# Zero-adding fillers on TensorE: 128 columns in a softmax bank instead of 256 in a free one, six softmax banks from the first unit, and another order

## The chip, the cores and the metric

The kernel runs on one core of one Trainium2 chip. The metric is the device time of one execution in microseconds (us), smaller being better. TensorE (PE in the profile) multiplies, VectorE (DVE) and ScalarE (ACT) do the element-wise work, GpSimd (POOL) builds masks, SyncE (SP) issues the DMAs. PSUM, where TensorE writes, has eight banks of 512 fp32 columns.

## The reference

Three layers on 4 batches of 576 tokens, 8 heads of 64:

```
scores = q k^T / 8, masked: heads 0-3 to the last 32 positions, heads 4-7 to every 32nd position
x  = softmax(scores) v                       (2304 x 512)
x  = mish(x w_in) w_out                      (512 -> 2048 -> 512)
out = max(x w1, x w2, x w3) w_out2           (512 -> 768 -> 512)
```

q and k come scaled up by 8, and the weights come in 64-bit words that the kernel turns into fp32 itself.

## The kernel before

Attention is cut into 48 units, 12 for each batch: a unit is three or four blocks of one pair of heads. Each unit has one PSUM bank for its whole life. It goes: mask by a matmul (`mask_mm`, L476, in the first two batches), scores (L485, 64x64 tiles of the array), row maximum on VectorE (L506), exponentials on ScalarE (L518), division on VectorE (L531), transposes on TensorE (L542), copies out of the bank (L554: for the strided heads one on ScalarE and one on VectorE, from different partitions of one bank into different columns of the same tile), the product with v (L563), and the split of the result into a high and a low part of x (L581 ScalarE, L585 VectorE). For the first batch, q and k are transposed on TensorE (L409, 96 columns each) and copied out (L422 ScalarE, L424 VectorE); later batches use VectorE (L382).

The first layer (L608, `h_mm`) starts on a block of tokens as soon as its x is there, so its matmuls lie between those of the attention units. Every product runs in three passes of high and low parts. x w_out follows (`x2_mm`, L641), then a Strassen scheme for the wide layers (L826) and the last product (L943).

The order on every engine is written out by a planner at build time. `Plan.add` notes each step with a cost, its reads and its writes; `Plan.run` simulates the engines with these costs and takes, whenever an engine is free, the ready step of the best rank. Twenty seeds shake the ranks one after the other. `START` says when each engine begins in the plan's time (ns).

**Fillers.** Where the plan's TensorE would stand idle, `Plan.run` (L196 to L203) puts in matmuls of zeros. It counts one as FILL columns at 2.4 or 1.2 GHz, as its own model of the clock says for that moment (`HAM`, `HAM_COLS`), and puts in as many as end `FILL_GAP` ns ahead of the next step. Fillers are no steps of the plan: they have neither reads nor writes there. In the built program the semaphores come from the tiles that the instructions touch.

**Banks.** `ATT_BANKS` are five banks that the units take in turn. The bank acc0 is the fillers' at first, and from unit 12 (`SIXTH`) on it is the sixth bank of the units, so that unit 17 is the first to use it. From the first step of such a unit that the plan takes, no more fillers are put in (`plan.unfilled`; `fill` in L198 stays false once it is false). At the start VectorE sets the zeros that the fillers read (L1268) and clears the five banks in the order a0, a1, a2, acc1, acc2 (L1270).

Of the kernel before, what the change touches and what calls it, by code (L numbers as in the profile page):

```python
# [21 lines left out]
P = 128  # L22
# [18 lines left out]
LQ = 64  # L41
LK = LQ + STRIDE
RES = 3
ATT_BANKS = ("a0", "a1", "a2", "acc1", "acc2")
RAW_BANKS = ("h0", "acc3")
RING = dict(h=3, g=5, ev=4, wt=4, hq=10, land=6, s=6, st=8, pt=3, raw=2, qT=2, v=2)
CFG = dict(lead_conv=2.43, att_rate=1.0, att_lead=0.53, start_conv=4.96, start_step=1.17, start_unit=1.19, x2=0.0)
PASSES = ((0, 0), (0, 1), (1, 0))

START = dict(pe=1460, act=1900, dve=4360, pool=5630, sp=1000, qa=1000)  # L50
WAIT = dict(
    pe=dict(pe=0, act=200, dve=210, pool=200, sp=200), act=dict(pe=260, act=140, dve=150, pool=200, sp=150),
    dve=dict(pe=230, act=140, dve=130, pool=160, sp=150), pool=dict(pe=260, act=200, dve=200, pool=130, sp=200),
    sp=dict(pe=200, act=160, dve=160, pool=160, sp=100),
)
for waits in WAIT.values():
# [4 lines left out]
ISSUE = dict(v_load=470, tr_ld=575)  # L61
QUEUE = 200
PIECES = dict(qk_load=36, tr_ld=36, w_first=32, w_load=32)
SIXTH = 12
HAM, HAM_COLS = 10240 / 3, 3060
SMALL_MM = ("scores", "tp", "av", "qkt")
MODE = dict(scores="64x64", tpq="64x64", avs="64x64", av="128x64")
SWITCH_IN, SWITCH_OUT, SWITCH_TILED = 140, 200, 145
STAY = 2000
TABLE = dict(exps="exp", mish="mish", mish1="mish")  # L70
TABLE_LOAD, TABLE_STAY = 1400, 4000
FILL, FILL_GAP = 256, 100
ROUNDS = 5
MOVED, JITTER = (0.01, 0.03, 0.1, 0.2), (1000, 2000, 4000)
SEEDS = (2000001, 2000002, 2000007, 2000010, 2000013, 2000055, 2000060, 2000065, 2000101, 2000130, 2000162, 2000272, 2000304, 2000349, 2000351, 2000592, 2001064, 2001088, 2001199, 2001207)
COST = dict(
    act=lambda n, psum=False, ptr=False: (51 if psum else 93) + n / 1.2 + (93 if ptr else 0),
    dve=lambda n, fast=False: 69 + n / (1.92 if fast else 0.96),
# [4 lines left out]
def switch(was, mode):  # L83
    if was == mode:
        return 0
    return SWITCH_IN if was is None else SWITCH_OUT if mode is None else SWITCH_TILED


def pieces(name, cost):
    return cost / 20 if name == "v_load" else PIECES.get(name, 16)  # L90


class Queued:

    def __init__(self):
        self.held, self.sum = deque(), 0
# [13 lines left out]
class Plan:  # L110
# [6 lines left out]
    def __init__(self, filler):  # L117
        self.filler = filler
        self.name, self.eng, self.cost, self.cols, self.rank, self.emit = [], [], [], [], [], []
        self.pred, self.succ = [], []  # L120
        self.writer, self.readers = {}, {}
        self.unfilled = set()

    def add(self, name, eng, cost, emit, reads=(), writes=(), rank=0.0, cols=0):
        i = len(self.name)
# [16 lines left out]
    def run(self, rank, backward):  # L142
        succ, pred = (self.pred, self.succ) if backward else (self.succ, self.pred)
        n = len(self.name)
        left = [len(p) for p in pred]
        ready, done = [0.0] * n, [0.0] * n
        free = dict.fromkeys(self.ENGINES, 0.0) if backward else dict(START)
        later = {e: [] for e in self.ENGINES}
        now_ready = {e: [] for e in self.ENGINES}
        for i in range(n):  # L150
            if not left[i]:
                heappush(later[self.eng[i]], (0.0, i))
        order, wire, busy, last, mode, fill, count = [], 0.0, {}, None, None, True, 0
        queued = {e: Queued() for e in self.ENGINES}
        table = "mish" if backward else "exp"
        while count < n:
            now, e = min(
                (free[e] if now_ready[e] else max(free[e], later[e][0][0]), j)
                for j, e in enumerate(self.ENGINES) if now_ready[e] or later[e]
            )  # L160
            e = self.ENGINES[e]
            while later[e] and later[e][0][0] <= now:
                i = heappop(later[e])[1]
                heappush(now_ready[e], (rank[i], i))
            if e == "pe" and last is not None:
                def worth(entry):
                    name = self.name[entry[1]]
                    same = MODE.get(name) == mode
                    return entry[0] - STAY * same, entry[1]

                r, i = min(now_ready[e], key=worth)
                now_ready[e].remove((r, i))
                heapify(now_ready[e])
            elif e == "act":
                def late(entry):
                    t = TABLE.get(self.name[entry[1]], table)
                    return entry[0] + TABLE_STAY * (t != table), entry[1]

                r, i = min(now_ready[e], key=late)
                now_ready[e].remove((r, i))  # L180
                heapify(now_ready[e])
            else:
                i = heappop(now_ready[e])[1]
            cost = self.cost[i]
            if e == "act":
                t = TABLE.get(self.name[i], table)
                cost += TABLE_LOAD * (t != table)
                table = t
            if e in ("sp", "qa"):
                now = max(now, queued[e].room(pieces(self.name[i], cost)))  # L190
                free[e] = now + ISSUE.get(self.name[i], DMA_ISSUE)
                wire = max(wire, now + (0 if backward else DMA_START)) + cost
                queued[e].put(wire, pieces(self.name[i], cost))
                done[i] = wire + (DMA_START if backward else 0) + DMA_END + LATE.get(self.name[i], 0)
            else:
                if e == "pe":  # L196
                    t, w = free[e], int(free[e] // HAM)
                    fill = fill and not backward and self.name[i] != "x2_mm" and i not in self.unfilled  # L198
                    while fill and t + (c := FILL / (2.4 if busy.get(w - 1, 0) >= HAM_COLS else 1.2)) + FILL_GAP <= now:
                        busy[w] = busy.get(w, 0) + FILL  # L200
                        order.append(-1)
                        t += c
                        w = int(t // HAM)  # L203
                    last, was, mode = self.name[i], mode, MODE.get(self.name[i])
                    cost += switch(was, mode)
                    if not backward:
                        w = int(now // HAM)
                        busy[w] = busy.get(w, 0) + self.cols[i]
                        cost *= 1 if busy.get(w - 1, 0) >= HAM_COLS else 2
                done[i] = free[e] = now + cost  # L210
            order.append(i)
            count += 1
            for j in succ[i]:
                wait = WAIT[self.eng[j]][e] if backward else WAIT[e][self.eng[j]]
                ready[j] = max(ready[j], done[i] + wait)
                left[j] -= 1
                if not left[j]:
                    heappush(later[self.eng[j]], (ready[j], j))
        return order, done, max(done)
# [10 lines left out]
    def order(self):  # L230
# [3 lines left out]
        rank = self.rank  # L234
        for seed in (*SEEDS, None):
            end, order, done = self.settle(rank, ROUNDS)
# [12 lines left out]
def build_plan(k, B, H, S, D, DM, FF, FF2, wide):  # L249

    plan = Plan(lambda: k.fill())
    add = plan.add
    nc = k.nc
# [10 lines left out]
    act, dve, mm = COST["act"], COST["dve"], COST["mm"]  # L264
# [166 lines left out]
    def unit(n, i, u, tiles, b, hp, local, r, rv):  # L431
        rk = unit_rank(n)
        nt = len(tiles)
# [1 line left out]
        C = LK if local else LQ  # L435
        M = LQ if local else RK
        rows = P if local else LQ + RK
        tag = ATT_BANKS[n % len(ATT_BANKS)] if n < SIXTH else (*ATT_BANKS, "acc0")[n % 6]
        bk = ("bank", tag)
        sb = ("s", ring("s"))  # L440
        pb = ("pt", ring("pt"))
# [20 lines left out]
                return a[:, st:st + LK]  # L462
            return a[:, NJ * RES * tl:NJ * RES * tl + width(tl)]

        if tag == "acc0":
            plan.unfilled.update(range(len(plan.name), len(plan.name) + nt + 1))
        on_pe = b < PE_MASK
        if on_pe:
            def mask_mm():
# [592 lines left out]
def sparse_attention_moe_kernel(  # L1062
# [13 lines left out]
    nc = tc.nc  # L1076
# [30 lines left out]
    for i in range(RING["g"]):  # L1107
# [14 lines left out]
    banks = {tag: psum.tile([P, 512], F32, name=f"bank_{tag}")  # L1122
             for tag in ("a0", "a1", "a2", "h0", "acc0", "acc1", "acc2", "acc3")}
# [125 lines left out]
    zero = x[:, 0, KC - 1, NT - FILL:]  # L1249

    def fill():
        nc.tensor.matmul(banks["acc0"][:, :FILL], lhsT=zero[:, :P], rhs=zero, start=True, stop=True)

    bufs = dict(work, s=s_t, pt=pt_t)
    env = SimpleNamespace(
        nc=nc, fill=fill, x=x, x2p=x2p, out=out, ident=ident, m_first=m_first, m_res=m_res, m_first_r=m_first_r, m_res_r=m_res_r, ident_r=ident_r,
        bank=lambda tag: banks[tag], wt=lambda r: wt[r][:], words=split_words,
        stage=lambda s: slot_tile(s, [P, 1024], U32), open_slot=lambda s: slot_tile(s, [P, 2, 512], F32R),
# [5 lines left out]
    plan = build_plan(env, B, H, S, D, DM, w_in.shape[1], w1.shape[1], wide)  # L1264
    order, _ = plan.order()
    with tc.manual_schedule():
        nc.scalar.preload_act_table_set("exp_and_others")
        nc.vector.memset(zero.bitcast(F32), 0.0)  # L1268
        for tag in ATT_BANKS:
            nc.vector.memset(banks[tag][:], 0.0)  # L1270
# [33 lines left out]
```

## Time and profile before

| | |
|---|---|
| median of 3 runs | 749.46 us (748.99 to 749.92) |
| the profiled execution | 747.73 us, its span 745.7 us |
| TensorE busy | 736.7 us (99%), 5192 matmuls |
| VectorE, ScalarE busy | 519.8 us (70%), 400.0 us (54%) |
| granted TensorE clock over the span | 0.994 |

All times inside the trace count from the start of the span. A matmul is busy from its issue until its last result is written, so consecutive matmuls overlap and a short stop of the array does not show as idle time. The granted clock is 1.00 at 2.4 GHz and 0.50 at 1.2 GHz.

### The profile page before, as it was taken

How to read it: one execution, taken by the hardware profiler on the slowest of the kernel's cores; microseconds unless marked ns; L12 is line 12 of the kernel's file. 1: busy time of each engine (PE TensorE's matmuls, PEld its weight loads, DVE VectorE, ACT ScalarE, POOL GpSimd, SP SyncE). 2: the span in 40 equal slices, each digit the busy share in tenths (PEclk: the TensorE clock that was granted, in tenths of full speed). 3: DMA queues.
4: the chain of work that ended last, by engine and by line, in shares of the span. 5: the costliest groups of instructions: out<-in, count | busy, mean ns of one | idle time of the engine just before them, and what ended most of it. 6: DMA issues, size and time to landing. Idle time of an engine off the chain costs nothing.

```text
span 745.7 us, 14087 instructions
## 1 busy us (share of the span) xinstructions
PE 736.7 (99%) x5192; PEld 707.3 (95%) x5192; DVE 519.8 (70%) x1174; ACT 400.0 (54%) x1082; POOL 6.0 (1%) x28
## 2 busy tenths in 40 slices
PE   8999999999999999999999999999999999999998
PEld 7799987999999999999999999999999999998886
DVE  5999997893798488333886769966656854694321
ACT  5868888695656266252663747543244343353331
POOL 3000000000000000000000000000000000000000
PEclk9999999999999999999999999999999999999999
DMA  9897783443555657345681326212520441365542
GB/s 192 167 159 134 136 165 102 167 156 115 178 155 185 196 190 251 99 126 169 211 270 44 127 74 211 85 58 68 167 68 28 131 131 57 116 203 169 177 130 85
DMA packets 152212, 105.39 MB, mean 141 GB/s; under 512 B 95312, under 2 KB 145488, under 8 KB 152144
## 3 DMA queue, kind: packets, MB, share of 16 engines
q1 hardware_dynamic: 150960, 104.20, 48.8%
q8 instruction: 41, 0.67, 0.4%
q10 hardware_dynamic: 1184, 0.30, 0.2%
q14 instruction: 27, 0.22, 0.1%
HBM read 74.58 MB, written 29.88 MB: 140 GB/s over the span
## 4 chain that ended last, share of the span: by engine, by line
PE 93%; DVE 3%; ACT 2%; DMA 1%; POOL 0%; issue 0%; SPq 0%; POOLq 0%; DVEq 0%; ACTq 0%
PE bank_acc L641 27%; PE bank_a L826 21%; PE bank_acc L826 11%; PE bank_h L826 11%; PE bank_acc L943 5%; PE bank_a L943 3%; PE bank_h L608 3%; PE bank_acc L608 3%; PE bank_acc L485 1%; PE bank_h L943 1%; PE bank_a L563 1%; PE bank_a L485 1%; ACT s L518 1%; PE bank_acc L563 1%; PE bank_a L542 1%; DMA rawk<-in_k_dram 1%
## 5 line engine op out<-in xcount | busy, mean ns | idle before, releaser
L641 PE MATMUL bank_acc<-g,wslot 128*128 128x384 f32 x1152 | 210.6, 334 | 0.0
L641 PEld LDWEIGHTS bank_acc<-g,wslot 128*128 128x128 f32 x1152 | 200.5, 188 | 0.1
L826 PE MATMUL bank_a<-x,wslot 128*128 128x384 f32 x732 | 143.3, 334 | 0.0
L826 PEld LDWEIGHTS bank_a<-x,wslot 128*128 128x128 f32 x732 | 128.4, 188 | 0.0
L333 ACT CAST wslot<-wt 128x512 fp32r<-128x512 f32 (+1 forms) x86 | 50.1, 584 | 31.6 <-DVE wt L319 21.7
L674 DVE SCALAR_TENSOR_TENSOR ev<-bank_acc,ev 128x384 f32<-128x384 f32 x72 | 39.0, 552 | 37.4 <-PE bank_acc L641 35.3
L826 PE MATMUL bank_acc<-ty,wslot 128*128 128x384 f32 x324 | 64.4, 334 | 0.0
L337 DVE TENSOR_TENSOR wslot<-wt,wslot 128x512 fp32r<-128x512 f32 (+1 forms) x86 | 53.8, 637 | 6.1 <-ACT wslot L333 5.9
L826 PEld LDWEIGHTS bank_acc<-ty,wslot 128*128 128x128 f32 x324 | 56.9, 188 | 0.1
L826 PE MATMUL bank_h<-ty,wslot 128*128 128x384 f32 x240 | 48.0, 334 | 0.0
L943 PE MATMUL bank_acc<-wslot,g 128*128 128x512 f32 x180 | 44.9, 389 | 0.0
L636 DVE TENSOR_TENSOR g<-h,g 128x384 fp32r<-128x384 f32 x45 | 24.7, 554 | 25.8 <-ACT g L635 25.5
L826 PEld LDWEIGHTS bank_h<-ty,wslot 128*128 128x128 f32 x240 | 42.2, 188 | 0.0
L309 DVE TENSOR_SCALAR wt<-wt 128x512 uint32<-128x512 uint32 x56 | 23.4, 421 | 24.8 <-ACT wt L305 24.7
L943 PEld LDWEIGHTS bank_acc<-wslot,g 128*128 128x128 f32 x180 | 33.8, 188 | 6.9
L313 DVE SCALAR_TENSOR_TENSOR wt<-wslot,wt 128x512 uint32<-128x512 uint32 x56 | 38.4, 686 | 0.7
L305 ACT ACTIVATE wt<-wslot 128x512 f32<-128x512 f32 x56 | 37.5, 676 | 2.1 <-DMA wslot<-in_moe_w_dram 1.8
L319 DVE SCALAR_TENSOR_TENSOR wt<-wslot,wt 128x512 uint32<-128x512 uint32 x56 | 38.0, 683 | 0.3
L826 PE MATMUL bank_h<-x,wslot 128*128 128x384 f32 x186 | 37.2, 334 | 0.0
L608 PE MATMUL bank_h<-x,wslot 128*128 128x288 f32 (+2 forms) x168 | 35.0, 334 | 0.0
L608 PE MATMUL bank_acc<-x,wslot 128*128 128x288 f32 (+2 forms) x168 | 34.0, 334 | 0.0
L842 ACT COPY bank_acc<-bank_a 128x384 f32<-128x384 f32 x27 | 12.6, 465 | 38.6 <-PE bank_a L826 38.3
(174 smaller groups left out, 1222.0 us busy)
## 6 DMA issues: line engine op xcount, KB each, us to landing
x2p<-ev SPq DMA_DIRECT2D x72, 192.0 KB
ev<-x2p SPq DMA_DIRECT2D x72, 192.0 KB
wslot<-in_moe_w_out_dram SPq DMA_DIRECT2D x22, 512.0 KB
wslot<-in_moe_w_dram SPq DMA_DIRECT2D x18, 512.0 KB
wslot<-in_moe_w_in_dram SPq DMA_DIRECT2D x16, 512.0 KB
ty<-t SPq DMA_DIRECT2D x20, 384.0 KB
h<-g SPq DMA_DIRECT2D x24, 192.0 KB
hy<-h SPq DMA_DIRECT2D x24, 192.0 KB
```

Of the source, the lines that this page charges most:

```text
L305: nc.scalar.mul(k.wt(r2).bitcast(F32), k.words(slot)[1].bitcast(F32), 2.0 ** -111)
L309: nc.vector.tensor_scalar(out=t, in0=t, scalar1=3, scalar2=None, op0=ALU.logical_shift_left)
L313: nc.vector.scalar_tensor_tensor(out=t, in0=k.words(slot)[1], scalar=0x80000000, in1=t, op0=ALU.bitwise_and, op1=ALU.bitwise_or)
L319: nc.vector.scalar_tensor_tensor(out=t, in0=k.words(slot)[0], scalar=29, in1=t, op0=ALU.logical_shift_right, op1=ALU.bitwise_or)
L333: nc.scalar.copy(out=k.open_slot(slot)[:, 0, :n], in_=k.wt(r2)[:, c0:].bitcast(F32))
L337: nc.vector.tensor_tensor(out=s[:, 1, :n], in0=k.wt(r2)[:, c0:].bitcast(F32), in1=s[:, 0, :n], op=ALU.subtract)
L608: nc.tensor.matmul(k.bank(hb)[:, :n], lhsT=wap(("in", f), a, c), rhs=k.x[:, q, c, t0:t0 + n], start=(c == 0 and m == 0), stop=(c == KC - 1 ...
L636: add("gl", "dve", dve(n), lambda: nc.vector.tensor_tensor(out=g()[:, 1, :n], in0=Hh(), in1=g()[:, 0, :n], op=ALU.subtract), reads=[h, G0] ...
L641: nc.tensor.matmul(k.bank(f"acc{c}")[:, :n], lhsT=wap(("out", f), a, c), rhs=g()[:, q, :n], start=(first and m == 0), stop=(last and m == 2),)
L674: add("x2_add", "dve", dve(n), (lambda c=c, e=e, ab=ab: nc.vector.scalar_tensor_tensor(out=k.work("ev", e)[:, :n], in0=k.bank(ab)[:, :n], ...
L826: nc.tensor.matmul(k.bank(bank)[:, :SP], lhsT=left(i, a, pa, j), rhs=operand(p, b, pb, j, x2), start=start and n == 0, stop=n == 5, skip_g ...
L943: nc.tensor.matmul(k.bank(ab)[:], lhsT=k.g(rg)[:, a, c * P:(c + 1) * P], rhs=t[:, q, :], start=(f == 0 and m == 0), stop=(f == F2C - 1 and ...
```

## The change

- A filler has 128 columns instead of 256 (`FILL`), and may end 60 ns instead of 100 ns ahead of the next step (`FILL_GAP`). It goes into columns 384 to 511 of the bank a2, with `start=False`, so that it adds zeros there. The units use at most the first 384 columns of a bank.
- acc0 is one of six `ATT_BANKS` from unit 0 on. `SIXTH` and `plan.unfilled` go, so fillers may be put in until the first `x2_mm`. Six banks are cleared at the start: a0, a1, a2, acc1, acc2, acc0.
- The zeros are set over 128 columns of x instead of 256.
- The plan begins TensorE at 1200 ns instead of 1460, and its model of the clock has another mark (`HAM_COLS`).
- Other seeds: the order of all steps is new.

```diff
-ATT_BANKS = ("a0", "a1", "a2", "acc1", "acc2")
+ATT_BANKS = ("a0", "a1", "a2", "acc1", "acc2", "acc0")
-START = dict(pe=1460, act=1900, dve=4360, pool=5630, sp=1000, qa=1000)
+START = dict(pe=1200, act=1900, dve=4360, pool=5630, sp=1000, qa=1000)
-SIXTH = 12
-HAM, HAM_COLS = 10240 / 3, 3060
+HAM, HAM_COLS = 10240 / 3, 3700
-FILL, FILL_GAP = 256, 100
+FILL, FILL_AT, FILL_GAP = 128, 384, 60
-SEEDS = (2000001, ...)
+SEEDS = (1000001, ...)
...
-                    fill = fill and not backward and self.name[i] != "x2_mm" and i not in self.unfilled
+                    fill = fill and not backward and self.name[i] != "x2_mm"
...
-        tag = ATT_BANKS[n % len(ATT_BANKS)] if n < SIXTH else (*ATT_BANKS, "acc0")[n % 6]
+        tag = ATT_BANKS[n % len(ATT_BANKS)]
...
-        if tag == "acc0":
-            plan.unfilled.update(range(len(plan.name), len(plan.name) + nt + 1))
...
     def fill():
-        nc.tensor.matmul(banks["acc0"][:, :FILL], lhsT=zero[:, :P], rhs=zero, start=True, stop=True)
+        nc.tensor.matmul(
+            banks["a2"][:, FILL_AT:FILL_AT + FILL], lhsT=zero, rhs=zero, start=False, stop=True, skip_group_check=True
+        )
```

## Rows read from the trace of the kernel before

**Rows 1.** Stretches: length, busy us of PE, PEld, DVE, ACT, POOL, clock, DMA, GB/s

```profile
14.00:34.00 20.00, 17.95 (x301) 14.35 (x300) 18.47 (x61) 18.22 (x91) 0.00 (x0) 1.00 0.98 179
34.00:42.00 8.00, 8.00 (x87) 7.22 (x88) 5.88 (x21) 3.63 (x15) 0.00 (x0) 0.57 1.09 204
42.00:140.00 98.00, 96.94 (x1342) 86.21 (x1341) 89.74 (x279) 81.85 (x355) 0.00 (x0) 1.00 0.67 135
140.00:700.00 560.00, 560.00 (x3197) 554.48 (x3197) 387.20 (x779) 277.41 (x577) 0.00 (x0) 1.00 0.43 140
```

**Rows 2.** Waits of TensorE, 10 to 41 us: us in total, times, longest

```profile
PE bank_a L542 <- ACT s L518: 0.7, 1, 0.7
...
PEld bank_a L476 <- DVE x L585: 0.4, 1, 0.4
...
PE bank_acc L485 <- ACT qTq L422: 0.2, 1, 0.2
```

**Rows 3.** Waits of TensorE, 41 to 140 us

```profile
PE bank_acc L485 <- DVE x L585: 0.4, 1, 0.4
...
PE bank_acc L485 <- DVE qTk L382: 0.2, 1, 0.2
```

**Rows 4.** Timeline of TensorE, 0 to 20 us: start, us, instruction, [idle before]

```profile
1.18 4.00 PE L1252 MATMUL bank_acc<-x 128*128 128x256 f32 x17 [1.18 <-DVE x L1268]
5.47 0.71 PE L409 MATMUL bank_h<-ident,earlyq 96*128 96x96 f32 x3 [0.29 <-POOL s L1151]
...
9.33 0.59 PE L476 MATMUL bank_acc<-m_first_r,ident_r 128*128 128x288 f32 x1
9.85 1.83 PE L485 MATMUL bank_a<-qTk,qTq 64*64 64x96 f32 x36
...
15.77 0.41 PE L409 MATMUL bank_h<-ident,earlyq 96*128 96x96 f32 x3
...
19.46 0.40 PE L476 MATMUL bank_a<-m_first_r,ident_r 128*128 128x288 f32 x1
```

**Rows 5.** Groups of TensorE, 0 to 10 us: xcount | busy us, mean ns

```profile
L476 PE MATMUL bank_a<-m_first_r,ident_r 128*128 128x288 f32 x3 | 1.4, 539 | 0.0
L476 PE MATMUL bank_acc<-m_first_r,ident_r 128*128 128x288 f32 x3 | 1.4, 539 | 0.0
```

**Rows 6.** Timeline of VectorE, the start

```profile
0.86 0.27 DVE L1268 MEMSET x<- 128x256 f32 x1 [0.86 <-PEq L1289]
1.23 1.56 DVE L1270 MEMSET bank_a<- 128x512 f32 x3
...
6.86 0.46 DVE L424 COPY qTk<-bank_acc 128x288 f32<-128x288 f32 x1 [2.98 <-PE bank_acc L409]
```

**Rows 7.** Groups of TensorE, 40 to 140 us

```profile
L608 PE MATMUL bank_acc<-x,wslot 128*128 128x128 f32 x12 | 1.5, 275 | 0.0
L608 PE MATMUL bank_h<-x,wslot 128*128 128x128 f32 x12 | 1.5, 270 | 0.0
```

**Rows 8.** Weight loads, 40 to 140 us and then 0 to 10 us

```profile
L608 PEld LDWEIGHTS bank_acc<-x,wslot 128*128 128x128 f32 x150 | 22.9, 189 | 1.7
...
L1252 PEld LDWEIGHTS bank_acc<-x 128*128 128x128 f32 x17 | 3.7, 328 | 1.2 <-DVE x L1268 1.2
```

**Rows 9.** Timeline of TensorE, around 62 us

```profile
61.06 0.60 PE L608 MATMUL bank_h<-x,wslot 128*128 128x288 f32 x3
61.59 0.61 PE L485 MATMUL bank_acc<-qTk,qTq 64*54 64x54 f32 x16
...
63.20 0.67 PE L608 MATMUL bank_h<-x,wslot 128*128 128x288 f32 x3
63.71 0.56 PE L608 MATMUL bank_acc<-x,wslot 128*128 128x288 f32 x3
```

**Rows 10.** Waits of VectorE and of ScalarE, 10 to 140 us

```profile
DVE pt L554 <- ACT pt L554: 1.8, 5, 0.5
...
ACT pt L554 <- DVE pt L554: 1.7, 5, 0.5
```

More of the change, by code (lines that the diff above doesn't have):

```diff
@@ L63 @@
 PIECES = dict(qk_load=36, tr_ld=36, w_first=32, w_load=32)
-SIXTH = 12
-HAM, HAM_COLS = 10240 / 3, 3060
-SMALL_MM = ("scores", "tp", "av", "qkt")
+HAM, HAM_COLS = 10240 / 3, 3700
 MODE = dict(scores="64x64", tpq="64x64", avs="64x64", av="128x64")
@@ L71 @@
 TABLE_LOAD, TABLE_STAY = 1400, 4000
-FILL, FILL_GAP = 256, 100
+FILL, FILL_AT, FILL_GAP = 128, 384, 60
 ROUNDS = 5
 MOVED, JITTER = (0.01, 0.03, 0.1, 0.2), (1000, 2000, 4000)
-SEEDS = (2000001, 2000002, 2000007, 2000010, 2000013, 2000055, 2000060, 2000065, 2000101, 2000130, 2000162, 2000272, 2000304, 2000349, 2000351, 2000592, 2001064, 2001088, 2001199, 2001207)
+SEEDS = (1000001, 1000002, 1000003, 1000004, 1000009, 1000077, 1000082, 1000087, 1000142, 1000168, 1000181, 1000185, 1000187, 1000190, 1000273, 1000333, 1000373, 1000500, 1000562, 1000593)
 COST = dict(
@@ L121, in __init__ @@
         self.writer, self.readers = {}, {}
-        self.unfilled = set()
     def add(self, name, eng, cost, emit, reads=(), writes=(), rank=0.0, cols=0):
```

## The prediction

> **What bounds the kernel now.** I read the table of stretches first [rows 1]. From 140 to 700 us TensorE has no idle time and the clock is full, and the change touches no step there; between 42 and 140 it is 99% busy. So the end comes when TensorE has done its list of work: whatever it loses or gains before 42 us is lost or gained at the end, as long as VectorE, 92% busy from 42 to 140 (89.74 of 98), can follow. Before 42 us there are two losses. From 14 to 34 us ScalarE and VectorE are the tight ones (18.22 and 18.47 of 20), and TensorE waits for them, six times by name between 10 and 41 us, 2.6 us in all [rows 2]. From 34 to 42 us TensorE is busy all the time, but at a mean clock of 0.57: (1 - 0.57) x 8 / 0.5 = 6.9 us at the lower of its two levels, 3.4 us of work lost, while VectorE is busy only 5.88 of 8. After 41 us TensorE waits three times, 1.0 us in all [rows 3].
>
> All 17 fillers lie between 1.18 and 5.18 us [rows 4]. The plan couldn't put in more after 9.33: five banks serve the first 12 units, but six masks have run by 10 us [rows 4, 5], and the sixth is that of unit 17 in acc0, the step that ends the filling. So the fillers do nothing for the clock that is low at 34.
>
> **Part by part.** *When the fillers can start.* Today the first filler follows the setting of its zeros, which ends at 1.13 us [rows 4, 6], since acc0 isn't cleared. The new filler adds to a2, the third bank that VectorE clears, and must come after that. The three a-banks take 1.56 us from 1.23 on [rows 6]; zeros over half the columns save some 0.14 us; so a2 is clear at 2.65 and the first filler runs at about 2.7. The sixth clearing costs nothing: VectorE is idle for 2.98 us after the fifth [rows 6].
>
> *How many there are.* Seventeen fillers of 213 ns from 1460, 100 ns kept free, put the first transposes of the plan between 5187 and 5400 (no further filler fitted). From 1200 on, at 107 ns, 60 kept free, that is 36 to 38. I take 37. The plan doesn't know of the 1.5 us by which they start late.
>
> *What one takes.* No row has a filler of 128 columns. The same shape (128x128 weights, 128 columns, the same number format) is in the first layer's last block: 12 in 1.5 us, of which one takes 0.275, so (1.5 - 0.275) / 11 = 111 ns from start to start at the full clock [rows 7], where 128 columns stream in 53. Something other than streaming sets the pace, the weight load by the looks of it, and that is slower too at the lower level: 328 ns against 189 [rows 8], 1.74 times. The transposes of 96 columns take 0.71 us for three at 5.47 and 0.41 at 15.77 [rows 4]; the 0.59 and 0.40 of the mask matmul at 9.33 and 19.46 say the same, that TensorE runs at the lower level until about 10 us (the table of stretches shows 1.00 there; the durations decide). Bounds for one filler at the start: 107 ns, the pace per column of today's fillers (256 columns at 1.2 GHz are 213 ns, 17 of them 3.6 of the 4.00 us, the rest is the way of the last one's results), and 222, twice the 111. I take 210, nearer the upper end, because both rows of the same work at both levels show a factor of 1.7 or more.
>
> The Trainium skill ("TensorE: Matmul & The Clock Gate", Back-to-back issue gap) gives about 81 ns for one matmul in a stream of loads and matmuls of 128 columns; the row has 111, and the row decides. By 81 the two terms for late fillers below would halve, and the sum would come out 1 us lower.
>
> *The start, summed.* 37 x 0.21 = 7.8; 2.7 + 7.8 = 10.5 us, and the first transposes, at 5.47 today, come 5.0 us late (1.3 at 111 ns each). Queued behind the fillers on TensorE is all of batch 0: no transpose, no scores, so no softmax on either engine. From there the stage up to 34 us is set by ScalarE and VectorE, which have 1.78 and 1.53 us of slack in 20 [rows 1]; if that slack takes 1.8, 3.2 us are left. Bounds: -0.5 (cheap fillers, clock up early) to +5.0. I take **+3.2**.
>
> *Fillers in the waits, 10 to 41 us.* The plan will see waits much like the six [rows 2] and fill them. It counts 53 ns for a filler that takes 111, so a wait filled with eight ends 8 x 0.058 = 0.46 us late. Six such are 2.8; nothing if the next step is late anyway. As ScalarE and VectorE set the pace here, I take **+1.0**.
>
> *Fillers after 41 us.* Here TensorE has no slack, and a filler that the plan puts where TensorE would in truth not wait costs itself whole, and, between 64x64 matmuls, a change of tiling there and back: three matmuls of 288 columns stream in 0.36 us, but the next scores start 0.53 after the first of them, and on the way back 0.51 pass [rows 9], so 0.17 and 0.15, ordinary steps included. Three waits are known [rows 3]: three runs at some 0.3 give **+1.0**. Bounds: 0, and 5.4 for a dozen runs with two fillers each (12 x 0.45).
>
> *Bank a2.* The two copies of one softmax bank wait for each other, 1.8 us in 5 times and 1.7 in 5 [rows 10], though they read other partitions and write other columns: the program puts accesses of two engines to one bank in order. So a filler waits for a read of a2 that is under way, and the unit's next read waits for the filler. Nine runs, a2 in use by one of the two engines about a third of the time, half of an operation of 0.3 to 0.5 each: 0.6 at most if all of it counted; I take **+0.4** (0 to 4.5, which is every run waiting 0.5).
>
> *The clock at 34 us.* If fillers close the waits at 32 us, the clock should hold. Gain at most 3.4; VectorE's idle 2.1 us from 34 to 42 bounds it below. I take **-2.5** (0 to -3.4).
>
> *The sixth bank.* A unit before 42 us waits once 0.4 us for its bank, the weight load of its mask [rows 2]; that goes: **-0.4**. Nothing else of batch 0 is seen to wait for a bank. In batches 1 to 3 the units have six banks already.
>
> *The new order and the model's marks* have no row; 0, with 1 us to either side.
>
> Sum: +3.2 + 1.0 + 1.0 + 0.4 - 2.5 - 0.4 = +2.7 us. The profiled execution took 747.73 (span 745.7 and 2.0 around it), so 750.4; the median of the runs lies 1.73 above it, at 749.46, so 752.2 there, 0.36% slower. Its own range, with the start between 1.5 and 5: 750.5 to 754.
>
> **Rivals.** *Faster, 747.3: fillers are cheap at the lower clock.* At 111 each, 37 end at 6.8 us, 1.3 late; TensorE, without a break from 2.7 on, is then at the full clock for transposes and masks, which take 2.4 instead of the 4.4 us from 5.47 to 9.85. Scores begin some 0.6 earlier, of which copies of 0.46 between the transposes leave 0.3. -0.3 + 1.0 + 1.0 + 0.4 - 2.5 - 0.4 = -0.8 with late fillers as above, -2.2 if these stay inside the waits as well (take 1.4 off the two terms). For it: 256 columns stream at full pace. Against: the 111. It decides from about 130 ns a filler downwards. Chance 0.24.
>
> *No change, 749.6: the clock rises among the start fillers.* If it does in the middle, 18 fillers take 3.8 from 2.7 on and 19 more 2.1, to 8.6; the transposes and masks then take 2.4, and scores begin at 11.0, 1.2 late; half is taken up: +0.6 + 1.0 + 1.0 + 0.4 - 2.5 - 0.4 = +0.1. For it: TensorE has no break from 2.7 on. Against it: the fillers from 1.18 to 5.18, without a break too, left the transposes behind them at the lower level. Chance 0.18.
>
> The Trainium skill ("TensorE: Matmul & The Clock Gate", Why this matters for your kernels) asks for continuous work on TensorE to reach the full clock, and by that rule it would be this rival that comes true; the transposes at 5.47 show that today's fillers alone didn't bring it in time.
>
> *Much slower, 756.6: many fillers after 41 us.* A dozen runs instead of three, 5.4 instead of 1.0. For it: with the filling at an end by 9.33, no row shows how often the plan sees short gaps there. Chance 0.10.
>
> *The fillers don't hold the clock, 754.7.* The waits that the plan fills are not those that happen, and the clock falls as before or elsewhere: 2.5 back. Chance 0.12.
>
> **Chances and range.** My forecast has 0.36. A measurement of this kernel can tell about 0.2%, 1.5 us. Slower: 0.36 + 0.10 + 0.12 = 0.58; same 0.18; faster 0.24. The range 746.8 to 756.6 leaves out the lower part of the faster case and the upper half of the much slower one, together some 0.18.
>
> **What would show it.** First filler at 2.7 and not 1.1 us, waiting for the clearing of a2; some 37 of them 210 ns apart; the first transposes at 10.5, the first scores near 15. No stretch below 1.00 between 14 and 42 us. Fillers 111 ns apart later on, in runs of about eight, TensorE's waits of 10 to 41 us shorter, and the next steps late. New waits of fillers for ScalarE or VectorE on a2. The forecast is wrong if the start fillers are less than 150 ns apart, if the transposes come before 8 us, or if scores that start 5 us late are made up for by 42 us.

## The result, and the profile after

The changed kernel takes 753.77 us (median of 6 runs, 752.10 to 755.05) against 749.23 before: a ratio of 1.007, 95% interval 1.0047 to 1.0093. The forecast was 752.2. Timed once more, beside three of the experiments:

> The changed kernel itself, on the same chip as the other three of this set: all of them are compared with it. Expected 3.5 to 5.5 us above before, ratio 1.005 to 1.009.

It took 753.21 (1.006, 1.0040 to 1.0079). The profiled execution of the first set took 753.42, with a span of 751.6.

The fillers by line, after (duration ns min/median/max, first and last start), and who waited for them:

```profile
L1247 PE MATMUL bank_a<-x x85: 234/305/476, 2.7 to 42.5; 128*128 128x128 f32 x85
...
  DVE bank_a L1267: 5.4, 2
  ACT s L513: 1.4, 2
who waited for it (us, times):
  ACT s L513: 1.2, 1
  ACT pt L549: 0.5, 1
```

There are 85 instead of 17. Of the later 47, 24 lie between 32.2 and 35.4 us, and the last eight on 42 us; none starts after 42.5. Three runs of them in the timeline of TensorE:

```profile
32.20 1.58 PE L1247 MATMUL bank_a<-x 128*128 128x128 f32 x13
...
34.01 1.43 PE L1247 MATMUL bank_a<-x 128*128 128x128 f32 x11
...
41.66 1.09 PE L1247 MATMUL bank_a<-x 128*128 128x128 f32 x8
```

The start, in the timelines of VectorE and of TensorE:

```profile
0.83 0.17 DVE L1265 MEMSET x<- 128x128 f32 x1 [0.83 <-PEq L1286]
1.10 1.56 DVE L1267 MEMSET bank_a<- 128x512 f32 x3
2.72 1.57 DVE L1267 MEMSET bank_acc<- 128x512 f32 x3
```

```profile
2.72 8.37 PE L1247 MATMUL bank_a<-x 128*128 128x128 f32 x38 [2.72 <-DVE bank_a L1267]
10.89 0.70 PE L406 MATMUL bank_h<-ident,earlyq 96*128 96x96 f32 x3
...
14.57 0.59 PE L471 MATMUL bank_acc<-m_first_r,ident_r 128*128 128x288 f32 x1
...
15.20 1.95 PE L480 MATMUL bank_a<-qTk,qTq 64*64 64x96 f32 x24
```

The first filler waits for the clearing of a2, 1.5 us later than in the kernel before [rows 4, 6]. The 38 take 8.37 us; less the 0.42 that the last one takes from its issue to its last result, (8.37 - 0.42) / 37 = 0.215 us each. The transposes start at 10.89 instead of 5.47 and the scores at 15.20 instead of 9.85 [rows 4], 5.4 us late. The mask at 14.57 still takes 0.59, as at the lower clock.

The stretches, after (columns as in [rows 1]):

```profile
14.00:34.00 20.00, 19.40 (x279) 17.14 (x279) 15.34 (x51) 15.84 (x75) 0.00 (x0) 1.00 0.94 179
34.00:42.00 8.00, 8.00 (x131) 7.31 (x129) 7.21 (x26) 6.90 (x35) 0.00 (x0) 1.00 0.99 196
42.00:140.00 98.00, 97.42 (x1388) 85.54 (x1388) 88.13 (x286) 81.90 (x361) 0.00 (x0) 1.00 0.65 133
140.00:700.00 560.00, 559.44 (x3206) 553.73 (x3205) 390.26 (x783) 276.22 (x578) 0.00 (x0) 1.00 0.43 139
```

The low clock of 34 to 42 us is gone, and VectorE and ScalarE do there what they didn't do from 14 to 34, where they are now less busy than in [rows 1]. From 42 us on the two kernels look alike: most of the loss was made before.

The following table is not a view of the profile. It is worked out from the records of the traces: the time (us) at which so many columns of real matmuls, fillers left out, had been issued. It shows where each kernel (the experiments are below) gains or loses on the others.

```
columns    before   after   no start  start    narrow start  clock held
                            fillers   fillers  in before     in before
                                      alone
  1000       7.07   12.31     6.96    12.31      10.78         6.96
  5000      10.78   16.70    11.35    16.43      13.92        10.82
 10000      15.06   22.02    16.68    20.58      18.20        15.09
 25000      27.84   35.93    30.57    33.79      31.00        27.88
 45000      44.37   48.70    43.35    47.89      47.41        42.15
 95000      71.79   76.58    71.24    75.76      74.83        71.61
195000     127.45  132.20   127.61   132.23     130.69       128.94
650000     335.33  340.20   335.57   340.20     338.58       336.83
end        745.71  751.64   746.39   751.14     749.96       747.40
```

After lies 5.2 us behind before at 1000 columns, 8.1 at 25000, 4.3 at 45000, 4.8 at 195000 and 5.9 at the end: lost at the start, 2 more lost between 10 and 36 us, nearly 4 given back where before ran at the low clock, and 1.6 lost in the 700 us after that.

### The profile page after: what moved, and what is told of

Read it like the earlier page. It is cut to its first block, busy times and chain, and to the rows that moved or that the text cites. A ratio compares the mean times of both kernels' runs of the same rounds, so it can differ in the third digit from the quotient of the medians.

```text
span 751.6 us, 14208 instructions
## 1 busy us (share of the span) xinstructions
PE 743.5 (99%) x5260; PEld 714.3 (95%) x5260; DVE 518.5 (69%) x1175; ACT 399.1 (53%) x1082; POOL 6.1 (1%) x28
## 4 chain that ended last, share of the span: by engine, by line
PE 90%; DVE 5%; ACT 3%; DMA 2%; issue 1%; SPq 0%; DVEq 0%; ACTq 0%
PE bank_acc L636 27%; PE bank_a L821 20%; PE bank_h L821 11%; PE bank_acc L821 10%; PE bank_acc L938 5%; PE bank_a L938 3%; PE bank_h L603 2%; PE bank_acc L603 2%; PE bank_a L1247 2%; ACT s L513 2%; PE bank_h L938 1%; DMA h<-g 1%; PE bank_acc L480 1%; PE bank_a L480 1%; PE bank_acc L558 1%; PE bank_a L558 1%
## 5 line engine op out<-in xcount | busy, mean ns | idle before, releaser
L821 PE MATMUL bank_acc<-x,wslot 128*128 128x384 f32 x162 | 32.4, 335 | 0.6 <-DVE h L841 0.6
L821 PEld LDWEIGHTS bank_h<-x,wslot 128*128 128x128 f32 x186 | 32.5, 188 | 0.3 <-DVE hy L841 0.2
```

Source lines behind the costliest of these rows:

```text
L821: nc.tensor.matmul(k.bank(bank)[:, :SP], lhsT=left(i, a, pa, j), rhs=operand(p, b, pb, j, x2), start=start and n == 0, stop=n == 5, skip_g ...
```

## The experiments

Each kernel was timed beside the kernel before, whose median in the three sets was 749.14, 748.94 and 749.21. Single runs of one kernel spread over 3 us and more, so medians and intervals decide here, and single profiles only show where the time lies.

**No start fillers.** The order and the 47 later fillers stay.

```diff
-        for emit in order:
-            emit()
+        at = 0
+        for emit in order:
+            if emit is plan.filler:
+                at += 1
+                if at <= 38:
+                    continue
+            emit()
```

> The changed kernel without the 38 fillers ahead of the first transposes; the 47 later ones and the order stay. Theory (the start fillers hold TensorE until 10.9 us and nothing makes that up): first transposes near 5.5 us, first scores near 10, time 4.5 to 6 us below the changed kernel, so 748 to 749.5 beside a before of about 749. Rival 1 (the new order or the six banks cost the time, the start is made up for by 42 us): within 1.5 us of the changed kernel, 752.5 or more. Rival 2 (the fillers at the start are what brings the clock up, and without them it stays low for longer): gain of 2 us or less, and scores at the lower pace beyond 13 us.

749.07 us; ratio 0.9998 (0.9979 to 1.0018): all of the loss is gone. The timeline of TensorE has the transposes and the scores where they were before:

```profile
5.37 0.71 PE L406 MATMUL bank_h<-ident,earlyq 96*128 96x96 f32 x3 [5.37 <-DMA earlyq<-in_q_dram]
...
9.22 0.59 PE L471 MATMUL bank_acc<-m_first_r,ident_r 128*128 128x288 f32 x1
...
9.85 2.06 PE L480 MATMUL bank_a<-qTk,qTq 64*64 64x96 f32 x24
```

The first rival falls: order and banks don't cost the time. So does the second: without any filler at the start TensorE reaches the scores as early as the kernel before with its 17.

**Start fillers alone** (`if at > 38: continue`), in two sets.

> The changed kernel with the 38 fillers of the start and without the 47 between 15 and 43 us. Theory (the later fillers cost about 2 us of TensorE between 25 and 36 us, but keep the clock up, worth up to 3.4): the clock falls once between 25 and 45 us, and the time is 0 to 2 us above the changed kernel, 753.5 to 755.5. Rival (the clock holds without them, as TensorE's work comes 5 us later and denser): no stretch below 1.00 and the time about 2 us below the changed kernel, 751.5 to 752.

> The changed kernel without the 47 later fillers once more, now beside the changed kernel on one chip. In its first profile it led the changed kernel by up to 2.1 us where 25000 columns of real work were done and lay behind it by 0.0 to 0.8 between 45000 and 175000, the clock having been low for 3.4 us. Theory (the later fillers cost about what the clock gives back): within 1 us of the changed kernel. Rival (they only cost): 1.5 to 2.5 us below it.

751.91 us (1.0033, 1.0013 to 1.0053), and 752.13 (1.0036, 1.0013 to 1.0059) beside 753.21 for the changed kernel. The first expectation had the time 0 to 2 us above the changed kernel; it lies 1.1 to 1.9 below. The later fillers do hold the clock: the 16 timed runs of the changed kernel have a granted clock of 0.999 or more over the span. Without them the windows from 24 to 46 us show it below 1.00, (0.11 x 12 + 0.04 x 10) / 0.5 = 3.4 us at the lower level:

```profile
24.00:36.00 12.00, 10.70 (x171) 8.82 (x166) 11.22 (x39) 11.55 (x56) 0.00 (x0) 0.89 0.80 164
36.00:46.00 10.00, 9.50 (x151) 7.99 (x151) 8.85 (x30) 6.75 (x31) 0.00 (x0) 0.96 0.78 142
```

By the table this kernel is 2.1 us ahead of the changed one at 25000 columns, 0.8 ahead at 45000 and level at 195000. (The second expectation has it behind there; the table does not.) The rival of the first expectation, that the clock holds by itself, is out for the profiles, but not for every run: 8 of the 24 timed runs have a granted clock of 0.999 or more and a median of 750.2 us, the other 16 have 752.4. Whether the later fillers are a small loss or nothing is left open: 1.1 us lie between the two medians, and the intervals overlap.

**No filler at all** (`if True: continue`).

> The changed kernel without any filler: order and six banks alone. Theory: first transposes near 5.5 us; both terms of the fillers are gone, the gain of the clock too: 748.5 to 750.5, near the kernel before. Rival (order and banks are worse by themselves): 752 or more. Rival (they are better, and only the fillers hide it): 747 or less.

750.51 us (1.0013, 0.9989 to 1.0036): near before, at the upper end of what was expected. Beside the kernel without start fillers this has the 47 later ones as a gain of 1.4 us, where the pair above had them as a loss of 1.1. Both are within what these runs can tell; neither sign is shown. Read the other way, the start fillers cost 1.4 to 1.6 us without the later ones (751.91 and 752.13 against 750.51) and 4.1 to 4.7 with them; the granted clock is below 0.999 in 11 of the 12 runs without any filler, and what this does to the difference was not separated.

**Nineteen start fillers of 256 columns, and nineteen of 128.** The first writes columns 256 to 511 of a2 before a unit has used it.

```diff
+    def fill_wide():
+        nc.tensor.matmul(
+            banks["a2"][:, 256:], lhsT=zero[:, :P], rhs=zero, start=False, stop=True, skip_group_check=True
+        )
...
+                if at <= 38:
+                    if at <= 19:
+                        fill_wide()
+                    continue
```

> The changed kernel with the 38 start fillers replaced by 19 of 256 columns, in the same bank, also adding; the 47 later ones stay at 128. As many columns of zeros, half as many weight loads. Theory (the weight load sets the pace, so 256 columns take the same 213 ns): fillers from 2.8 to 6.9 us, first transposes near 6.9, time 3.5 to 4.5 us below the changed kernel, 749 to 750.5. Rival (adding to a bank, or that bank, is what slows them, per column): 427 ns each, transposes at 10.9 as now, time unchanged at 753 to 754.

> The changed kernel with 19 start fillers of 128 columns instead of 38, the later ones kept. Theory (each takes 213 ns, and what counts is how late they let the first transposes start): fillers from 2.7 to 6.8, first transposes near 6.9, about 4 us earlier than now; time 3 to 4 us below the changed kernel. On the clock: with 19 fillers of 256 columns it rose at 7.8; if half the columns in the same time do less for it, it rises later, past 11 us, and the scores start 1 us later than there. Rival (unbroken work counts, not columns): it rises at about 8 us here too.

750.27 us (1.0019, 0.9996 to 1.0043) and 750.33 (1.0005, 0.9980 to 1.0031). TensorE of the wide ones, then of the narrow ones:

```profile
2.85 4.42 PE L1252 MATMUL bank_a<-x 128*128 128x256 f32 x19 [2.85 <-DVE bank_a L1272]
7.07 0.68 PE L406 MATMUL bank_h<-ident,earlyq 96*128 96x96 f32 x3
...
7.89 0.38 PE L471 MATMUL bank_a<-m_first_r,ident_r 128*128 128x288 f32 x1
...
9.98 1.21 PE L480 MATMUL bank_a<-qTk,qTq 64*64 64x96 f32 x24
```

```profile
2.72 4.32 PE L1247 MATMUL bank_a<-x 128*128 128x128 f32 x19 [2.72 <-DVE bank_a L1267]
6.83 0.70 PE L406 MATMUL bank_h<-ident,earlyq 96*128 96x96 f32 x3
...
7.72 0.59 PE L471 MATMUL bank_a<-m_first_r,ident_r 128*128 128x288 f32 x1
...
10.08 0.41 PE L406 MATMUL bank_h<-ident,earlyq 96*128 96x96 f32 x3
...
10.65 1.21 PE L480 MATMUL bank_a<-qTk,qTq 64*64 64x96 f32 x24
```

Nineteen take 4.42 us with 256 columns and 4.32 with 128. At the lower clock a filler costs the same with 128 columns as with 256; and adding to a2 slows nothing, as the 38 of 128 columns below take 8.37 us in acc0 too. The mask behind the wide ones takes 0.38, so the clock was up there, and 0.59 behind the narrow ones. Behind these it was up at 10.08, between the two moments of the expectation (past 11, or about 8), and the scores start 0.7 us later than behind the wide ones; but see the last section before reading that as what the columns do. What does set the pace, the weight load or another cost of each instruction, was not separated.

**a2 cleared first.**

```diff
-        for tag in ATT_BANKS:
+        for tag in ("a2", "a0", "a1", "acc1", "acc2", "acc0"):
```

> The changed kernel with a2 cleared first instead of third; all 85 fillers kept. Theory (the fillers wait for the clearing of a2, and every us that they start earlier is a us at the end): first filler at 1.7 instead of 2.7, first transposes at 9.8 instead of 10.9, time 1.05 us below the changed kernel. Rival (the start is not what the end hangs on): no change.

752.61 us (1.0049, 1.0030 to 1.0067), 0.6 below the changed kernel beside it. The start moved as expected:

```profile
1.64 8.37 PE L1247 MATMUL bank_a<-x 128*128 128x128 f32 x38 [1.64 <-DVE bank_a L1267]
9.81 0.70 PE L406 MATMUL bank_h<-ident,earlyq 96*128 96x96 f32 x3
```

So the wait for the clearing is real, 1.08 us of it. The 0.6 in the medians goes the expected way, but the two intervals overlap.

**The narrow start in the kernel before.** 38 fillers of 128 columns in acc0 for the 17 of 256; order, banks and all else stay.

```diff
+    def fill_narrow():
+        nc.tensor.matmul(
+            banks["acc0"][:, 384:], lhsT=zero[:, :P], rhs=zero[:, P:], start=True, stop=True, skip_group_check=True
+        )
...
+            if emit is plan.filler:
+                at += 1
+                if at == 1:
+                    for _ in range(38):
+                        fill_narrow()
+                continue
```

> The kernel before with its 17 start fillers of 256 columns replaced by 38 of 128, in acc0 (no clearing to wait for); nothing else changes, its order least of all. Theory (the length of the start fillers alone costs the time): fillers from 1.2 to 9.3 us, first transposes near 9.4 instead of 5.5, clock up one step later, time 3.5 to 4.5 us above before, 752.5 to 753.5. Rival (the loss needs the new order or the bank a2): within 1 us of before.

752.74 us (1.0044, 1.0023 to 1.0064): 3.5 us slower, with nothing else of the change.

```profile
1.18 8.37 PE L1255 MATMUL bank_acc<-x 128*128 128x128 f32 x38 [1.18 <-DVE x L1273]
9.35 0.70 PE L409 MATMUL bank_h<-ident,earlyq 96*128 96x96 f32 x3
...
13.12 1.70 PE L485 MATMUL bank_a<-qTk,qTq 64*64 64x96 f32 x36
```

The scores start 13.12 - 9.85 = 3.3 us late, and the table has 3.0 to 3.2 of it from 10000 to 195000 columns. Nothing makes it up.

**The clock held in the kernel before.** Sixteen fillers, in a bank that nobody reads then (`fill_narrow` with `start=False`).

```diff
+            at += name == "tp"
+            if name == "tp" and at in (16, 23):
+                for _ in range(8):
+                    fill_narrow()
             emit()
```

> The kernel before with 16 more fillers of 128 columns in the unused end of acc0: eight ahead of the transposes that wait at 24.2 us and eight ahead of those that wait at 32.3. Nobody reads acc0 there, so they wait for nobody. Theory (the clock that falls at 34 costs what I priced, 2.1 to 3.4 us, and 0.9 us of fillers in a wait of 0.9 cost nothing): no stretch below 1.00 before 700 us, time 2 to 3 us below before, 746 to 747. Rival (what the low clock costs is made up for by 175 us, as the changed kernel with and without its later fillers suggests): clock at 1.00, time within 1 us of before. Rival (16 are too few): the clock still falls.

748.06 us (0.9981, 0.9958 to 1.0004). The clock holds, in the profile and, at 0.997 or more, in all 12 timed runs. The fillers cost next to nothing where they lie: the transposes that waited start at 24.22 and 32.50, against 24.18 and 32.29 before.

```profile
23.29 1.09 PE L1255 MATMUL bank_acc<-x 128*128 128x128 f32 x8
24.22 0.50 PE L542 MATMUL bank_a<-ident,s 128*96 128x128 f32 x3
...
31.56 1.11 PE L1255 MATMUL bank_acc<-x 128*128 128x128 f32 x8
32.50 0.39 PE L542 MATMUL bank_acc<-ident,s 118*118 118x118 f32 x2
```

```profile
14.00:34.00 20.00, 19.50 (x318) 16.13 (x316) 18.49 (x61) 18.23 (x91) 0.00 (x0) 1.00 0.94 171
34.00:42.00 8.00, 7.95 (x113) 6.97 (x115) 7.81 (x25) 5.29 (x23) 0.00 (x0) 1.00 0.92 180
42.00:140.00 98.00, 95.40 (x1310) 83.57 (x1307) 86.29 (x273) 80.06 (x346) 0.00 (x0) 1.00 0.67 135
```

By the table it leads before by 2.2 us at 45000 columns, by 0.2 at 95000, and in this profile is 1.5 behind at 195000. (The profiled execution took 749.26, 1.2 above the median.) Its waits for DMAs from 42 to 140 us show where the lead went (us in total, times, longest):

```profile
DVE qTk L382 <- DMA rawk<-in_k_dram: 2.3, 4, 0.8
...
DVE qTq L382 <- DMA rawq<-in_q_dram: 1.4, 2, 0.8
...
PE bank_acc L563 <- DMA v<-in_v_dram: 1.2, 3, 0.6
```

Before has the first of these with 0.7 in one wait there, and no other for a DMA of 0.2 us or more. TensorE comes earlier, and the loads of q, k and v for the next batches don't: between 33 and 60 us SyncE issues every one of them 0.2 to 2.0 us later than in before. The same load in before, then here:

```profile
39.37 0.40 SPq L1239 DMA_DIRECT2D v<-in_v_dram  x1
```

```profile
41.35 0.40 SPq L1239 DMA_DIRECT2D v<-in_v_dram  x1
```

Why they are issued later, and whether other executions show it, stays open. The median is the best of all kernels here, but above the 746 to 747 that were expected, and its interval takes in 1: no version is shown to beat the kernel before.

The runs of the kernel before say more of what the clock is worth. Their granted clock over the span differs from run to run. Of the 103 in the three sets, 18 have 0.998 or more and a median of 747.5 us; 72 have 0.990 to 0.997 and 749.2; 13 have less and 753.7. So some 1.7 us of a clock that holds are still there at the end in this kernel. Nothing was changed between these runs, and what else differed is not known.

**The start of before in the changed kernel**: 17 fillers of 256 columns in the bank h0, which nobody clears, with all 47 later ones, and with every second of these (the last two added lines stand in the second kernel alone).

```diff
+    def fill_first():
+        nc.tensor.matmul(banks["h0"][:, :256], lhsT=zero[:, :P], rhs=zero, start=True, stop=True)
...
+                if at <= 38:
+                    if at <= 17:
+                        fill_first()
+                    continue
+                if at % 2:
+                    continue
```

> The changed kernel with the start of the kernel before: 17 fillers of 256 columns in the bank h0, which nobody clears, instead of 38 of 128 in a2; the 47 later ones stay. Theory (all of the loss is the start): first transposes at 5.5 us, time 4 to 5.5 us below the changed kernel, 747.5 to 749, same as before or a little below. Rival (a2 as the later fillers' bank and the new order cost something too): 750 or more.

> The same with 23 of the 47 later fillers, every second one left out. Theory (13 and 11 of them take 2.7 us between 32 and 36 us, longer than the waits that they were put into): 0.5 to 1 us below the kernel with all 47, if the clock holds. Rival (half of them no longer hold the clock): it falls once near 30 us, and the time is the same or up to 1.5 us above.

749.65 us (1.0001, 0.9978 to 1.0023) and 749.21 (1.0002, 0.9980 to 1.0024). The first lies between what theory and rival expected. With the start of before, the rest of the change is worth nothing that can be measured. 23 later fillers do as well as 47 in the median. They hold the clock in the profile, but not in every run: 5 of the 12 have a granted clock of 0.993 to 0.995, where the kernel with all 47 has none below 0.998.

## Why the prediction came out

**Direction and size** were right: +2.7 us forecast, +4.3 to +4.5 measured, inside the range.

**The start** went as worked out, nearly to the number: first filler at 2.72 (2.7 said), 38 of them (37), 0.215 us each (0.210), transposes at 10.89 (10.5), scores at 15.20 (near 15). That this is the loss is shown from both sides: without the start fillers the changed kernel is at before's time, and with them before is 3.5 us slower. The rival of cheap fillers falls with the 0.215. The rival of a clock that rises among them falls with the mask at 14.57. The term itself was too small: I let 1.8 us of ScalarE's and VectorE's slack take up part of a delay of 5.0 and put +3.2; the medians give 749.07 against 753.21 and 753.77, so 4.1 to 4.7, and the profiles 5.2. Slack inside the stage covered little of a start that was late as a whole: in the kernel before, 3.0 to 3.2 of the 3.3 us are left from 10000 to 195000 columns.

The Trainium skill ("TensorE: Matmul & The Clock Gate", LDWEIGHTS) puts a load at its columns / 1.2, for 128 columns an estimate of 107 ns. The 111 ns from start to start of [rows 7] at the full clock is near it, though the profile lists one load from its start to its end with 189 [rows 8]. The 0.215 us at the lower clock is twice the estimate, and the measured one is what the start costs.

**Fillers in the waits**, +1.0: 39 before 41 us, in six runs of 1 to 13. They put TensorE 2.1 us back at 25000 columns against the kernel that lacks them, twice the term; by 195000 nothing of it is left, the gain of the clock that they hold included.

**Bank a2**, +0.4: one place shows it, and the waits there are longer than the term. TensorE and ScalarE of the changed kernel, near 20 us:

```profile
19.69 1.11 PE L1247 MATMUL bank_a<-x 128*128 128x128 f32 x8 [0.60 <-ACT s L513]
```

```profile
19.17 0.37 ACT L513 ACTIVATE s<-bank_a,st 128x96 f32<-128x96 f32 x1
19.40 0.24 ACT L513 ACTIVATION_READ_ACCUMULATOR s<-bank_a,st 128x1 f32 x1
20.84 0.34 ACT L513 ACTIVATE s<-bank_a,st 128x96 f32<-128x96 f32 x1 [1.20 <-PE bank_a L1247]
```

Eight fillers wait for an exponential that reads a2, run, and only then may the next exponential of that unit read a2: ScalarE stands for 1.20 us. What this costs at the end was not measured by itself. The mechanism was foreseen. I priced half an operation for each run of fillers and left out that the next reader waits for the whole run.

**Fillers after 41 us**, +1.0: one run of eight, at 41.66, instead of three, and none after 43 us. It takes 1.0 us up to the next scores, at 42.68; what it costs at the end was not separated. The rival of many fillers there falls.

**The clock**, -2.5: it held, as said, and the rival that it wouldn't falls. Its worth was put too high. I argued that what TensorE gains before 42 us is gained at the end as long as VectorE can follow. In the kernel before with the clock held, 2.2 us are gained at 45000 columns, as priced, and in the profile go to waits for q, k and v. The medians leave 1.15 of it, not told apart from 0, and the runs of the kernel before that kept the clock are 1.7 ahead of those at 0.990 to 0.997. I had looked at one engine for the next limit and not at the loads.

**Sixth bank and order**, -0.4 and 0: alone, without any filler, they have 750.51 against 749.14, whose interval takes in 1; no gain is to be seen.

So the start was 0.9 to 1.5 us too small. All other terms together were put at -0.5; with no start fillers, or with those of before, the medians have them between -0.1 and +0.4. Within these the clock was 0.8 to 1.4 too favourable, and what the later fillers cost to set against it was not measured apart: that their sum came near is in part luck.

## What to carry to other kernels

Price a filler from a row of the same shape, start to start, and at the clock at which it will run; columns divided by the clock gave half or less of it here. Where a planner places fillers by a wrong price and without their waits, those ahead of the first real step can delay the whole program, as they did here, so count them up to the step behind them. And before a gain early in a kernel is booked at the end, look at the transfers of the next stage as well as at the engines: in the one profile here, waits for them took back what the clock gave.

## What the runs showed of the hardware

At the start the clock rose at different moments in kernels whose TensorE had done nearly the same until then. With the same 17 fillers of 256 columns from 1.18 us on, the first mask took 0.59 us in the kernel before with the clock held, and 0.38 in the changed kernel with that start, which reached its scores 0.9 us sooner. Until the first transposes the work of TensorE differs in the fillers' bank alone; the kernels around it differ in more:

```profile
6.42 0.59 PE L476 MATMUL bank_a<-m_first_r,ident_r 128*128 128x288 f32 x1
...
9.73 1.98 PE L485 MATMUL bank_a<-qTk,qTq 64*64 64x96 f32 x36
```

```profile
5.91 0.38 PE L471 MATMUL bank_a<-m_first_r,ident_r 128*128 128x288 f32 x1
...
8.79 1.21 PE L480 MATMUL bank_a<-qTk,qTq 64*64 64x96 f32 x24
```

The kernel with every second later filler has 0.38 there too. In the changed kernel TensorE has no idle time from 2.72 us on, and the mask at 14.57 still takes 0.59; the second profile of the same kernel has 0.59 at 14.58. So two executions of one kernel agreed, and two kernels did not. What decides was not tried; until it is, one profile of a start says little about what its fillers did to the clock. That holds for the wide and the narrow nineteen above as well.
